# Chunked retention, a Strassen down product and 64-column matmul pairs in a fused retention + feed-forward kernel

## Chip, cores and metric

The kernel runs on one core of a Trainium2 chip. The metric is the device time in microseconds (us) of one execution. Only fast runs are compared (a run counts as slow when it is more than 1.5% above the fastest of the same kernel). Profiles show a span, from the first to the last instruction; where both are known for one execution, the timed value lies about 2 us above it.

Each result was timed against runs of the kernel before on the same chip, in the same rounds. A ratio is the mean time of one kernel's fast runs over the mean of the other's of the same rounds, so it is not quite the ratio of the medians that are quoted. Medians of different calls come from different chips; the kernel before had medians of 455.5, 454.2, 451.2 and 450.1 us in the four sets of rounds, so differences under about 1% between sets are not read.

## The reference

Eight batches, eight heads, 576 positions, head size 64; then a feed-forward block over 4,608 tokens of width 512 with 2,048 hidden units. All inputs and the output are float32. The product `g` is called the gate below.

```python
scores = scale * q @ k.T                       # per batch and head, 576 x 576
gamma  = 1 - 2.0 ** (-5 - arange(8))           # one per head
D      = where(i >= j, gamma ** (i - j), 0)    # causal decay
x      = ((scores * D) @ v)                    # to (4608, 512)
h      = x @ w_in                              # (4608, 2048)
g      = h * clip(h + 3, 0, 6) / 6
out    = g @ w_out                             # (4608, 512)
```

## The kernel before

Attention is quadratic. For each batch and pair of heads, q and k are loaded with a cast to fp16, transposed on TensorE (PE), and multiplied into a causal 576-wide triangle, which the Vector engine (DVE) multiplies by a precomputed decay mask. ACT is the Scalar engine, POOL the GpSimd engine, SP the engine whose queue issues stores and, in the changed kernel, most loads. In both kernels PE's outputs are tiles in the memory PSUM, and the other tiles lie in the memory SBUF. Feed-forward "units" are popped between the attention pieces to keep PE busy.

```python
# feed-forward, for a block of 512 tokens
for dmc in range(NCC):                                   # 4, up product (line 122)
    nc.tensor.matmul(ph, win16[:, dmc, P*fc:P*fc+P], xt16[:, dmc, tok0:tok0+512], ...)
nc.scalar.activation(u, ph, Relu, bias=0.5, scale=1/6)
nc.vector.scalar_tensor_tensor(out=gt16[:, fc, :], in0=u, scalar=1.0, in1=ph, op0=min, op1=mult)
...
for fc in range(NFC):                                    # 16, down product (line 136)
    nc.tensor.matmul(pout, gt16[:, fc, P*mc:P*mc+P], wout16[:, fc, :], ...)
nc.scalar.copy(osb, pout)
...
# attention, one pair of heads
nc.tensor.transpose(pst[...], nat[0:sj, j, :], ident16)  # q and k, 5 each (line 174)
nc.tensor.matmul(pms[h2][0:mt, ...], kt2[64*h2:64*h2+64, ...], qt2[64*h2:...])   # line 200
nc.vector.tensor_tensor(out=at16s[h2][...], in0=pms[h2][...], in1=dmask[...], op=mult)  # line 210
nc.tensor.matmul(pos[h2][64*h2:64*h2+64, ...], vn16[...], at16s[h2][...])        # line 230
```

The shape of the PE tile follows from the operands: lines 122, 136 and 174 use all 128 rows and 128 columns, line 200 uses 64 rows (two heads side by side), line 230 uses 64 columns.

## Time and profile before

| | kernel before |
|---|---|
| time | 455.52 us, median of 2 (454.57 to 456.48) |
| profiled span | 448.7 us |
| PE / DVE / ACT / POOL busy | 88% / 51% / 45% / 40% |
| feed-forward matmuls | 1,152 of 512 columns, one each 216 ns = 249 us |
| changes of PE tile shape | 381; at an estimated 96 ns each, 37 us |

These lines are from the page of the kernel before: the busy time of each engine, then PE's and the DMA engines' busy share in 40 slices (a digit is tenths), the DMA packets, the chain of work that ended last, and the largest group of matmuls (busy time, mean ns of one).

```profile
span 448.7 us, 6207 instructions
...
PE 394.0 (88%) x2368; PEld 181.7 (40%) x2368; DVE 230.5 (51%) x432; ACT 201.6 (45%) x349; POOL 177.6 (40%) x222
...
PE   0387999989998999899998999899989999899996
...
DMA packets 134700, 29.73 MB, mean 66 GB/s; under 512 B 126480, under 2 KB 130064, under 8 KB 134672
...
PE 69%; DVE 18%; ACT 9%; issue 2%; POOL 1%; DVEq 0%; POOLq 0%
...
L122 PE MATMUL ph<-xt_104,win_102 128*128 128x512 f16 x576 | 143.2, 383 | 5.7 <-DVE gt_1_955 L128 0.8
```

PE bounds the kernel, but 88% busy is not 88% useful. A matmul's 383 ns is a latency; what counts is the distance between starts, 216 ns for 512 columns. On the chain of work that ended last, DVE and ACT stand for a quarter of the span. The next lines, PE's timeline of the kernel before (start, duration, line, operation, count), show a loss that no share shows.

```profile
204.51 1.24 PE L122 MATMUL ph<-xt_104,win_102 128*128 128x512 f16 x5
205.68 0.31 PE L230 MATMUL po_2133<-at16a,vn_2048 128*64 128x288 f16 x1
205.69 0.31 PE L230 MATMUL po_2134<-at16b,vn_2048 128*64 128x288 f16 x1
```

The last of the five matmuls of line 122 starts at 205.37 (four times 216 ns after 204.51). The next start should be at 205.59 but is at 205.68: the tile shape changed from 128*128 to 128*64 and PE lost about 95 ns. The Trainium skill, "TensorEngine Tiling (Array Packing)", Key Properties, says that changing the tiling mode drains the engine; the trace agrees and gives the price. The second thing to see is that the two 64-column matmuls at 205.68 and 205.69 run at the same time, one in each half of the array's columns.

### The profile page before, as it was taken

The numbers are of one execution on the slowest core, as the hardware profiler recorded it, in microseconds if no ns is written. First come the engines' busy times: TensorE is split into PE (matmuls) and PEld (weight loads), VectorE is DVE, ScalarE is ACT, GpSimd is POOL, SyncE is SP. The second block draws the span as 40 slices with busy tenths as digits, with TensorE's granted clock in tenths as the row PEclk, the third lists the DMA queues.
The fourth block names the chain that finished last, engine by engine and source line by source line (L and its number), as shares of the span: only waits on it lengthen the run. The fifth ranks groups of instructions, "written<-read, shape, count | busy, mean of one in ns | idle before, by whom it ended". The sixth has DMA issues, their size and how long they took to land.

```text
span 448.7 us, 6207 instructions
## 1 busy us (share of the span) xinstructions
PE 394.0 (88%) x2368; PEld 181.7 (40%) x2368; DVE 230.5 (51%) x432; ACT 201.6 (45%) x349; POOL 177.6 (40%) x222
## 2 busy tenths in 40 slices
PE   0387999989998999899998999899989999899996
PEld 0133444434443444444443444344443444344442
DVE  0254675347716672467635771667245763480540
ACT  5623564156522663356415652266325641571641
POOL 9966799763534444155326353445200000000000
PEclk9999999999998999999999999999998999999999
DMA  5999999985777766487568568776210001001101
GB/s 36 123 189 192 120 96 96 154 75 37 46 92 88 46 45 61 86 55 50 37 101 74 39 44 93 87 50 42 39 70 1 0 1 70 26 0 48 47 23 70
DMA packets 134700, 29.73 MB, mean 66 GB/s; under 512 B 126480, under 2 KB 130064, under 8 KB 134672
## 3 DMA queue, kind: packets, MB, share of 16 engines
q0 software_dynamic: 129488, 19.91, 60.8%
q1 hardware_dynamic: 5184, 9.44, 5.7%
q8 instruction: 18, 0.29, 0.3%
q14 instruction: 10, 0.08, 0.1%
HBM read 39.80 MB, written 9.44 MB: 110 GB/s over the span
## 4 chain that ended last, share of the span: by engine, by line
PE 69%; DVE 18%; ACT 9%; issue 2%; POOL 1%; DVEq 0%; POOLq 0%
PE pout L136 28%; PE ph L122 22%; DVE at16a L210 8%; DVE at16b L210 6%; PE pst L174 5%; ACT dmask L80 3%; ACT xt_104 L236 2%; ACT u L126 2%; ACT sb L180 2%; DVE gt_6_3580 L128 1%; DVE gt_5_3055 L128 1%; DVE gt_0_430 L128 1%; DVE gt_4_2530 L128 1%; DVE gt_3_2005 L128 1%; DVE gt_2_1480 L128 1%
## 5 line engine op out<-in xcount | busy, mean ns | idle before, releaser
L122 PE MATMUL ph<-xt_104,win_102 128*128 128x512 f16 x576 | 143.2, 383 | 5.7 <-DVE gt_1_955 L128 0.8
L126 ACT ACTIVATE u<-ph,cb 128x512 f32<-128x512 f32 x144 | 97.2, 687 | 53.2 <-PE ph L122 51.0
L122 PEld LDWEIGHTS <-win_102 128*128 128x128 f16 x576 | 52.6, 97 | 71.0 <-issue 19.5
L140 ACT COPY osb<-pout 128x512 f32<-128x512 f32 x36 | 21.1, 585 | 111.5 <-PE pout L136 111.5
L178 DVE COPY sb<-pst 128x576 f16<-128x576 f16 x32 | 14.5, 455 | 43.3 <-PE pst L174 43.3
L200 PEld LDWEIGHTS <-sb 64*128 64x128 f16 (+1 forms) x384 | 14.9, 100 | 42.5 <-ACT sb L180 18.2
L180 ACT COPY sb<-pst 128x576 f16<-128x576 f16 x32 | 20.4, 637 | 3.6 <-PE pst L174 1.6
L128 DVE SCALAR_TENSOR_TENSOR gt_8_4320<-u,ph 128x512 f16<-128x512 f32 x16 | 11.0, 688 | 16.6 <-ACT u L126 16.6
L128 DVE SCALAR_TENSOR_TENSOR gt_6_3580<-u,ph 128x512 f16<-128x512 f32 x16 | 10.7, 681 | 9.0 <-ACT u L126 8.9
L128 DVE SCALAR_TENSOR_TENSOR gt_2_1480<-u,ph 128x512 f16<-128x512 f32 x16 | 10.5, 679 | 9.2 <-ACT u L126 9.2
L128 DVE SCALAR_TENSOR_TENSOR gt_5_3055<-u,ph 128x512 f16<-128x512 f32 x16 | 10.7, 681 | 8.0 <-ACT u L126 7.8
L128 DVE SCALAR_TENSOR_TENSOR gt_4_2530<-u,ph 128x512 f16<-128x512 f32 x16 | 10.7, 681 | 8.0 <-ACT u L126 7.8
L128 DVE SCALAR_TENSOR_TENSOR gt_0_430<-u,ph 128x512 f16<-128x512 f32 x16 | 10.5, 680 | 8.3 <-ACT u L126 8.3
L128 DVE SCALAR_TENSOR_TENSOR gt_1_955<-u,ph 128x512 f16<-128x512 f32 x16 | 10.5, 680 | 8.1 <-ACT u L126 8.1
L128 DVE SCALAR_TENSOR_TENSOR gt_3_2005<-u,ph 128x512 f16<-128x512 f32 x16 | 10.5, 680 | 8.1 <-ACT u L126 8.1
L136 PE MATMUL pout<-wout_103,gt_2_1480 128*128 128x512 f16 x64 | 14.3, 379 | 0.2 <-DVE at16a L210 0.2
L136 PE MATMUL pout<-wout_103,gt_4_2530 128*128 128x512 f16 x64 | 14.3, 379 | 0.2 <-DVE at16a L210 0.2
L136 PE MATMUL pout<-wout_103,gt_0_430 128*128 128x512 f16 x64 | 14.3, 379 | 0.2 <-DVE at16a L210 0.2
L136 PE MATMUL pout<-wout_103,gt_1_955 128*128 128x512 f16 x64 | 14.3, 379 | 0.2 <-DVE at16a L210 0.2
L136 PE MATMUL pout<-wout_103,gt_5_3055 128*128 128x512 f16 x64 | 14.3, 379 | 0.2 <-DVE at16a L210 0.2
L136 PE MATMUL pout<-wout_103,gt_6_3580 128*128 128x512 f16 x64 | 14.3, 379 | 0.2 <-DVE at16a L210 0.2
L136 PE MATMUL pout<-wout_103,gt_3_2005 128*128 128x512 f16 x64 | 14.3, 379 | 0.2 <-DVE at16a L210 0.2
(1059 smaller groups left out, 775.9 us busy)
## 6 DMA issues: line engine op xcount, KB each, us to landing
out_dram<-osb SPq DMA_DIRECT2D x36, 256.0 KB, 2.0
win_102<-in_moe_w_in_dram POOLq DMA_DIRECT2D x2, 640.0 KB, 8.8
wout_103<-in_moe_w_out_dram POOLq DMA_DIRECT2D x2, 640.0 KB, 10.0
win_102<-in_moe_w_in_dram POOLq DMA_DIRECT2D x1, 768.0 KB, 9.9
wout_103<-in_moe_w_out_dram POOLq DMA_DIRECT2D x1, 768.0 KB, 10.5
qn_108<-in_q_dram POOLq DMA_DIRECT2D x2, 80.0 KB, 3.0
kn_109<-in_k_dram POOLq DMA_DIRECT2D x2, 80.0 KB, 3.0
vn_110<-in_v_dram POOLq DMA_DIRECT2D x2, 80.0 KB, 3.1
```

What stands on the lines that cost most here:

```text
L80: nc.scalar.activation(dmask[:, h, :], rsel, ACTF.Exp, bias=cb[:, 1:2], scale=float(np.log(gamma[h])))
L122: nc.tensor.matmul(ph, win16[:, dmc, P * fc:P * fc + P], xt16[:, dmc, tok0:tok0 + MBLK], start=(dmc == 0), stop=(dmc == NCC - 1))
L126: nc.scalar.activation(u, ph, ACTF.Relu, bias=cb[:, 0:1], scale=1.0 / 6.0)
L128: nc.vector.scalar_tensor_tensor(out=gt16[:, fc, :], in0=u, scalar=1.0, in1=ph, op0=ALU.min, op1=ALU.mult)
L136: nc.tensor.matmul(pout, gt16[:, fc, P * mc:P * mc + P], wout16[:, fc, :], start=(fc == 0), stop=(fc == NFC - 1))
L140: nc.scalar.copy(osb, pout)
L174: nc.tensor.transpose(pst[:, P * j:P * j + sj], nat[0:sj, j, :], ident16[0:sj, 0:sj])
L178: nc.vector.tensor_copy(sb, pst)
L180: nc.scalar.copy(sb, pst)
L200: nc.tensor.matmul(pms[h2][0:mt, co:co + ns], kt2[base:base + D, P * tcix:P * tcix + mt], qt2[base:base + D, a:bb], start=True, stop=True)
L210: nc.vector.tensor_tensor(out=at16s[h2][0:mtg, alo:alo + wid], in0=pms[h2][0:mtg, 0:wid], in1=dmask[0:mtg, 2 * c + h2, alo:alo + wid], op= ...
L236: nc.scalar.copy(xt16[h2 * D:h2 * D + D, c, b * S + s0:b * S + s1], pos[h2][h2 * D:h2 * D + D, 0:s1 - s0])
```

## The change

Five things change at once:

1. **Attention by chunks.** 128 tokens of one batch are a unit, and consecutive units come from different batches. A unit multiplies only its own 128 x 128 scores; the past enters through a 64 x 64 state per head, updated once per unit. The decay becomes factors on q and v and a constant mask.
2. **Loads and transposes.** q, k, v come as fp32 by hardware-issued DMA in rows of 256 B and are cast on POOL (those of the first four units partly on DVE and ACT). From unit 8 on the transposes are DMA transposes.
3. **Strassen (Winograd's form) for the down product.** Seven half-size products per block (M1 to M7 in the code) instead of eight, with fp16 sums on DVE and evictions on ACT, DVE and POOL.
4. **Pairs.** Each 128-column matmul of the up and down products is issued as two matmuls of 64 columns, so nearly everything on PE has the tile shape 128*64.
5. **A fixed order** of events by steps. Each step holds one up group (128 hidden units of one block: four products of 512 columns), at most one half of a Strassen product, and on average a quarter of an attention unit.

The core of the diff, with cuts marked (`at_t(t, f)` puts the piece of work `f` at step `t`):

```diff
+    def mm2(o, l, r, start, stop):
+        for hf in (0, 64):
+            mm(o[hf:hf + 64], l[:, hf:hf + 64], r, start, stop)
...
-            nc.gpsimd.dma_start(dst[:, :, coloff:coloff + D], ap)          # cast to fp16
+                eng.dma_start(t[p0:p0 + nr], src[b, :, P * c:P * c + nr, :]
+                              .rearrange("h s d -> s h d"))                # fp32, on SP
...
+        nc.sync.dma_start_transpose(qT[u]..., qpad[u % NQ]...)
+        nc.sync.dma_start_transpose(kT[u], k16[u]...)
...
+    def pu(u):                                   # state update
+                mm(ps[64 * a:64 * a + 64, pr], k16[u][:, h], v16[u][:, h], pr == 0, True)
...
-                nc.tensor.matmul(pout, gt16[:, fc, P * mc:P * mc + P], wout16[:, fc, :], ...)
+    PROD = ["M1", "M2", "M4", "M6", "M5", "M7", "M3"]
+    def down(n, hp):                             # half hp % 2 of product hp // 2
+        tag = {"M1": "A", "M6": "A", "M7": "A", "M2": "B", "M4": "B", "M5": "D", "M3": "D"}[m]
+        new = m in ("M1", "M2", "M4", "M5")
+            acc[tag] = psum.tile([P, 2, 256], FP32, tag="acc" + tag, bufs=1, ...)
+        for j in range(8):
+            mm2(ps[:, mt], a[:, j, P * mt:P * mt + P], w[:, j, :], ...)
+        if m == "M2":
+            V(out=osb[n][0][:, :, 0:256], in0=ps, in1=snap["M1"], op=ALU.add)
...
+    DSTART = 24                                  # step of the first down product
+        if u >= 7:
+            at_t(tu - 9 - LEAD, lambda u=u: load(u))                       # LEAD = 10
```

## The prediction

> **What bounds the kernel now.** TensorE. The page's busy line gives PE 88% of a 448.7 us span; the chain of waits gives PE 69%, DVE 18%, ACT 9%. PE's busy share hides three things. (a) Successive matmul starts show the feed-forward part (1,152 matmuls of 512 columns) running at 216 ns each, 249 us: already full rate. (b) Whenever consecutive matmuls change the tile shape, the next start comes about 96 ns late (a 512-column matmul is followed after 312 ns instead of 216): 381 changes, about 37 us. This agrees with the Trainium skill, "TensorEngine Tiling (Array Packing)", Key Properties: changing the tiling mode drains the engine. (c) In each 48.4 us batch, PE waits for the retention chain (mask multiply of 0.68 us on DVE, copies on ACT): about 54 us over the run. The start is slow too: the first score matmul runs at 19 us.
>
> **What the change does to PE.**
> - Up product: 576 pairs of two 64-column tiles at 512 columns. Two column tiles already run concurrently in this trace (288-column pairs start 3 to 6 ns apart and follow after 122 to 126 ns), so 216 ns a pair: 124 us, unchanged.
> - Down product: Strassen, 7 products for 8: 9×14×8 = 1,008 pairs of 256 columns; estimate 256/2.4+3 = 109 ns: 110 us instead of 124.
> - Attention: chunk states replace the 576-wide triangle: per 128-token unit 8 score, 8 state and 16 output matmuls, about 1.1 us when paired, 40 us for 36 units; it was about 60 us plus drains. DMA transposes replace PE's from unit 8 on.
> - All work but the first 8 units' transposes has one tile shape, so nearly all drains go.
> PE sum: about 280 us.
>
> Doubling the weight loads should not bind: 64-column loads take 106 to 112 ns of latency against 97, but are prefetched; PE's sequencer already sustains load+matmul every 56 ns (transposes), 28 ns an instruction, and a down pair needs 4 per 109 ns. This is the tightest margin.
>
> **Other engines (estimates from the trace).** DVE: 144 gates × 0.68 = 98, 72 masks × 0.68 = 49, 72 Strassen sums of 1,024 fp16 elements, perhaps 0.6 each = 43, evictions and states 30, start 15: about 235 us, plus waits for the SBUF port that it shares with POOL (the skill's "SBUF — State Buffer", "SBUF: two separate sides"; not shown by this trace) of perhaps 25. ACT about 145. POOL about 190. So DVE runs some 80 to 90% busy in the steady part and will cause some PE stalls. DMA: 110,000 packets of 256 B; this trace sustains about 770 small packets/us: 145 us plus weights, outputs and transposes; not binding afterwards, but binding at the start: seven units and w_in share one queue, so up-projection should stall for late w_in parts and full pace comes only near 55 to 60 us.
>
> **Sum.** 58 (start, 16 up steps) + 128 steps × 1.9 us (240) + last 14 half products and store 17 = 315, plus 5% waits = 328 span; the timed value lies 7 us above the span before: **335 us, range 300 to 385**. Faster by over 2%: 0.95; within: 0.02; slower: 0.03.
>
> **Right or wrong would show as:** pair spacing of 216 (up) and 109 ns (down); 312 ns drain gaps gone; a thin PE row until about 55 us; PE over 85% busy thereafter, idle ended mostly by DVE; a final 14-us stretch without up work.
>
> **What would make it wrong:** pairs not concurrent at 256 columns, or PE bound by issuing four instructions a pair (down at 200 ns adds 90 us); DVE's fp16 sums at one element a cycle or blocked by POOL (adds 30 to 60); DMA transposes queued behind loads starving scores; single accumulators making PE wait for DVE in each block.

## The result, and the profile after

| | before | after |
|---|---|---|
| time, median of 2 | 455.52 us | 346.41 us (346.37 to 346.46) |
| ratio of fast runs, 95% interval | 1 | 0.764 (0.750 to 0.777) |
| span | 448.7 us | 344.8 us |
| PE / DVE / ACT / POOL busy, us | 394 / 231 / 202 / 178 | 297 / 239 / 150 / 162 |
| mean granted PE clock | 0.991 | 0.945 |
| DMA packets | 134,700 | 166,830 |

The page of the changed kernel, the lines that answer to those above, with the row of PE's granted clock and that of the DMA engines:

```profile
span 344.8 us, 10257 instructions
...
PE 297.1 (86%) x4352; PEld 235.8 (68%) x4352; DVE 238.6 (69%) x392; ACT 150.1 (44%) x235; POOL 162.4 (47%) x228
...
PE   3663929776999989999998999999999999999881
...
PEclk9965876989899999999999999999999999999997
DMA  9999999999998599899689979949999801100305
...
DMA packets 166830, 55.72 MB, mean 162 GB/s; under 512 B 158080, under 2 KB 160128, under 8 KB 166784
...
PE 65%; DVE 13%; DMA 9%; POOL 5%; issue 4%; ACT 2%; SPq 1%; DVEq 0%; POOLq 0%
...
L53 PE MATMUL up<-xt,win 128*64 128x512 f16 x1152 | 154.7, 390 | 2.3 <-DVE gt L283 2.3
```

PE's row shows three parts: ten uneven slices (86 us) in which the clock row dips and the DMA row stands at 9, then a full stretch, then a short end. The DMA row stays high after the start too (the share is 0.90 from step 24 to 122), so the row alone doesn't show that DMA bounds the start; runs 3 and 4 look into that. Measured in the steps of the schedule, by the first matmul of each up group in the trace:

| up step begins at, us | 0 | 16 | 24 | 122 | 143 | span ends |
|---|---|---|---|---|---|---|
| changed kernel | 33.4 | 66.7 | 83.2 | 284.2 | 321.2 | 344.8 |

The distances between single matmul starts are as forecast. The two halves of an up pair start 31 ns apart and the next pair follows 185 ns later, 216 in all; of a down pair 31 and 78, 109 in all.

So the total fits. Whether it fits for the forecast reasons is another matter. From step 24 to step 122 the trace lets one compare what PE had to stream with what it took: summing columns/2.4 ns over all matmuls (half for a 64-column one) gives 187.1 us of array time, in 201.0 us. (The 2.4 columns per ns is an estimate from the two spacings: 256 columns more take 216 - 109 = 107 ns more.) I call a start late when it comes over 15 ns after (columns/2.4 + 5) ns from the start before it, and sum the excess as "gaps": 8.7 us here, of which 6.7 lie in front of down products, and 4.95 in front of matmuls into the accumulator B alone. One of these gaps, in three timelines of the changed kernel (PE, DVE, POOL):

```profile
180.56 1.06 PE L53 MATMUL up<-xt,win 128*64 128x512 f16 x8
...
181.94 0.25 PE L53 MATMUL O<-qT,X 128*64 128x128 f16 x2
183.47 0.74 PE L53 MATMUL accB3M<-tw,gt 128*64 128x256 f16 x10 [1.28 <-DVE osb L350]
```

```profile
179.58 1.27 DVE L220 TENSOR_TENSOR at<-sc,maskc 128x512 f16<-128x512 f32 x2
180.78 1.45 DVE L295 TENSOR_TENSOR su<-gt 128x1024 f16<-128x1024 f16 x1
182.15 0.68 DVE L283 SCALAR_TENSOR_TENSOR gt<-u,up 128x512 f16<-128x512 f32 x1
182.74 0.68 DVE L350 TENSOR_TENSOR osb<-accB3M,snap3M 128x512 f32<-128x512 f32 x1
```

```profile
180.63 1.04 POOL L184 TENSOR_TENSOR v<-stgv,gv 128x512 f16<-128x512 f32 x1
```

M4 is the product that follows M2 and begins on the same single-buffered accumulator. It has to wait until DVE has read M2's result at line 350. DVE came late to that because its queue held two masks, an fp16 Strassen sum and a gate. And the sum took 1.45 us where such a sum takes 0.68: POOL was running, and the sum ended 0.55 us after POOL's record did. Of the 72 sums of this kind, 51 took 0.70 us or less and 21 took over 0.75, up to 1.53; all 21 began while a POOL operation ran, and they ended 0.55 us after it (the extra sums to 10.5 us). Of the other 51 only four began during a POOL operation, in its last 0.15 us. The Trainium skill, "SBUF — State Buffer", "SBUF: two separate sides", says that a DVE operation with two SBUF inputs and a POOL operation that reads SBUF exclude each other for a whole instruction; the trace agrees.

### The profile page after: what moved, and what is told of

It reads as the page before. It is cut to its first block, busy times and chain, and to the rows that moved or that the text cites. A ratio compares the mean times of both kernels' runs of the same rounds, so it can differ in the third digit from the quotient of the medians.

```text
span 344.8 us, 10257 instructions
## 1 busy us (share of the span) xinstructions
PE 297.1 (86%) x4352; PEld 235.8 (68%) x4352; DVE 238.6 (69%) x392; ACT 150.1 (44%) x235; POOL 162.4 (47%) x228
## 2 busy tenths in 40 slices
DMA packets 166830, 55.72 MB, mean 162 GB/s; under 512 B 158080, under 2 KB 160128, under 8 KB 166784
## 4 chain that ended last, share of the span: by engine, by line
PE 65%; DVE 13%; DMA 9%; POOL 5%; issue 4%; ACT 2%; SPq 1%; DVEq 0%; POOLq 0%
PE up L53 27%; DMA stgk<-in_k_dram 6%; PE sc L53 3%; DMA kT<-k 3%; PE O L53 3%; DVE su L295 2%; DVE at L220 2%; DVE gt L283 2%; PE tp L205 2%; POOL qpad L182 2%; PE accA8M L53 2%; PE accA6M L53 2%; PE accA2M L53 2%; PE accA7M L53 2%; PE accA4M L53 2%
## 5 line engine op out<-in xcount | busy, mean ns | idle before, releaser
L282 ACT ACTIVATE u<-up,cb 128x512 f32<-128x512 f32 x144 | 98.9, 687 | 136.8 <-PE up L53 129.4
L53 PE MATMUL up<-xt,win 128*64 128x512 f16 x1152 | 154.7, 390 | 2.3 <-DVE gt L283 2.3
L283 DVE SCALAR_TENSOR_TENSOR gt<-u,up 128x512 f16<-128x512 f32 x144 | 98.2, 683 | 64.6 <-ACT u L282 64.2
L53 PEld LDWEIGHTS <-win 128*64 128x64 f16 x1152 | 76.4, 113 | 31.7 <-issue 7.8
L53 PEld LDWEIGHTS <-su 128*64 128x64 f16 x1152 | 65.3, 110 | 9.5 <-issue 4.2
L53 PEld LDWEIGHTS <-gt 128*64 128x64 f16 x864 | 49.7, 111 | 11.7 <-issue 7.0
L220 DVE TENSOR_TENSOR at<-sc,maskc 128x512 f16<-128x512 f32 x64 | 41.0, 681 | 5.6 <-PE sc L53 5.6
L184 POOL TENSOR_TENSOR v<-stgv,gv 128x512 f16<-128x512 f32 x36 | 38.4, 1066 | 11.2 <-DMA stgv<-in_v_dram 11.1
L182 POOL TENSOR_TENSOR qpad<-stgq,gq 128x256 f16<-128x256 f32 x64 | 40.8, 658 | 0.0
L295 DVE TENSOR_TENSOR su<-gt 128x1024 f16<-128x1024 f16 x36 | 29.9, 831 | 0.0
L53 PE MATMUL O<-qT,X 128*64 128x128 f16 (+1 forms) x256 | 16.4, 213 | 0.0
```

Of the source, the lines that this page charges most:

```text
L53: nc.tensor.matmul(o, l, r, start=start, stop=stop, skip_group_check=True)
L182: eq.tensor_tensor(out=qp[:, :, a, 64 * a:64 * a + 64], in0=s[:, :, a, :], in1=bc(ga), op=ALU.mult)
L184: ev.tensor_tensor(out=v16[u], in0=stg["v", u], in1=bc(gv), op=ALU.mult)
L220: nc.vector.tensor_tensor(out=at[u][:, 2 * hf:2 * hf + 2].rearrange("p c a s -> p (c a) s"), in0=ps.rearrange("p c a s -> p (c a) s"), in1 ...
L282: nc.scalar.activation(ut, ph, ACTF.Relu, bias=cb[:, 0:1], scale=1.0 / 6.0)
L283: nc.vector.scalar_tensor_tensor(out=gt[n][:, fc, :], in0=ut, scalar=1.0, in1=ph, op0=ALU.min, op1=ALU.mult)
```

## Experiments

Two theories stood against each other.

- **A:** PE bounds the kernel from step 24 on, and DMA bounds it before. The chunked attention, without drains, is most of the gain; Strassen gives its 14 us of PE time; pairs give the drains.
- **B:** The saving of Strassen is lost to its own sums and accumulators; the start is bound by engines; the pairs cost as much as they save.

The answer is a mix of the two. In the tables "stretch" is up step 24 to 122, "array" and "gaps" as defined above. All three are worked out from the starts of single matmuls in the run's trace.

### 1. No pairs (e1_nopair)

```diff
-    PAIR = True
+    PAIR = False
```

> The changed kernel with each 128-column product of the up and down parts as one matmul again instead of two 64-column tiles (half the matmuls and weight loads there). Theory A, pairing pays only by avoiding drains: the attention matmuls stay 64 columns wide, so each of the 32 units from the fifth on brings 4 changes of tile shape, 128 in all at 96 ns (the figure of the kernel before): 12 us slower, about 358 us, ratio to the changed kernel 1.03 to 1.04; spacing of up and down matmuls unchanged at 216 and 109 ns. Rival B, the doubled loads (weight loads 68% busy) slow PE: same or faster, 335 to 346. Rival C, two tiles stream faster than one 128-column matmul: much slower, over 375.

Measured: 352.88 us (351.01 to 354.76), ratio to before 0.782 (0.776 to 0.788). Slower than the changed kernel by 6.5 us by the medians, by some 8 by the ratios (0.782 against 0.764): half to 70% of the 12 us that theory A expected. Spacing is unchanged at 216 and 109 ns, so neither rival holds: two tiles do not stream faster, and the doubled weight loads do not slow PE. PE's timeline of this run shows the drain that the pairs avoid:

```profile
148.00 1.03 PE L53 MATMUL up<-xt,win 128*128 128x512 f16 x4
148.96 0.63 PE L53 MATMUL sc<-qT,kT 128*64 128x256 f16 x8
149.52 1.05 PE L53 MATMUL accA2M<-wout,gt 128*128 128x256 f16 x8
```

The four up matmuls would let the score start at 148.86; it starts at 148.96, and 25 such starts come 309 ns after the last up matmul instead of 216. The stretch grows by 5.7 us at the same array time (187.1), not by the 9.4 us of 98 drains (24.5 units, four changes each). In front of accumulator B the gaps even fell (4.95 to 3.99): drains in front of down products fell partly where PE was waiting for DVE already.

### 2. Plain down product (e2_plain_down)

```diff
-            at_t(d + hp, lambda n=n, hp=hp: down(n, hp), 3)
-            ... ssum(...), wsum(...)                       # all fp16 sums
+            at_t(d + hp, lambda n=n, hp=hp: plain(n, hp), 3)
+    def plain(n, hp):
+        for x in range(64 * hp // 14, 64 * (hp + 1) // 14):
+            mt, fc = divmod(x, 16)
+            # one bank per 128 tokens, rotating over accA, accB, accD
+            mm2(acc["p"], gt[n][:, fc, P*mt:P*mt+P], wout16[:, fc, :], fc == 0, fc == 15)
+            if fc == 15: nc.scalar.copy(osb[n][mt // 2][:, mt % 2, :], acc["p"]); ...
```

The gate tile gets a third buffer, in the space of the sums, because a plain product keeps it longer.

> The changed kernel with the plain down product (64 pairs of 512 columns a block, spread over the same 14 slots, evicted by four copies on ACT, third gate buffer) in place of Strassen's; no fp16 sums. Theory A, PE bounds the steady part: 9 blocks times (64*216 - 112*109 ns = 1.6 us) = 14.6 us more PE work, so 8 to 15 us slower than the changed kernel, 354 to 361 us, with DVE busy falling by about 80 us. Rival B, Strassen's sums and evictions on DVE and its single accumulators cost as much as they save: within 1.5% of the changed kernel or faster. The final stretch without up work grows from about 16 to about 15+2 us.

Measured: 344.28 us (342.61 to 344.88), ratio 0.763 (0.758 to 0.768), against 0.764 for the changed kernel. Theory A fell: Strassen's seven products are no faster than eight plain ones. The two stretches side by side; each line gives the window, its length, then busy us and count for PE, weight loads, DVE, ACT and POOL, then PE clock, DMA share and GB/s. The first is of the changed kernel:

```profile
83.20:284.20 201.00, 195.44 (x3064) 162.32 (x3065) 159.01 (x249) 94.47 (x149) 111.37 (x140) 0.99 0.90 169
```

and this one of the plain form:

```profile
83.40:286.10 202.70, 201.92 (x2421) 120.42 (x2419) 104.87 (x171) 94.43 (x149) 92.01 (x134) 1.00 0.88 170
```

| | stretch | array | gaps |
|---|---|---|---|
| Strassen, as changed | 201.0 | 187.1 | 8.7 |
| plain | 202.7 | 198.4 | 1.0 |

The plain form streams 11.3 us more and takes 1.7 us more. DVE is busy 54 us less, and PE waits for almost nothing. The end is also longer with Strassen: the last up group is followed by 23.6 us, in the plain form by 19.6 (323.6 to 343.2). Whatever Strassen saves is given back in those two places. What remained open was whether it had to be.

### 3. Same bytes in larger packets (e3_big_packets)

```diff
-                eng.dma_start(t[p0:p0 + nr], src[b, :, P * c:P * c + nr, :]
-                              .rearrange("h s d -> s h d"))
+                eng.dma_start(t[p0:p0 + nr] as (p, 512),
+                              contiguous 2 KB per partition from the same batch)
```

The result is wrong (relative error 1.4): the bytes are the right ones in the wrong places.

> Wrong results on purpose: the q, k, v chunk loads read the same bytes as contiguous rows of 2 KB per partition instead of 8 rows of 256 B, so the same bytes come in an eighth of the packets. Theory A, the start is DMA-bound by packets (now one 1,024-packet load lands every 1.15 us and the first down matmul runs at 85.8 us): first down matmul at 60 to 70 us, total 322 to 332 us, steady spacing (29.4 us for 14 steps) unchanged. Rival B, the start is bound by engines (POOL casts, PE clock after idling): first down matmul still after 80 us, total above 340.

Measured: 335.33 us (334.77 to 336.18), ratio 0.744 (0.739 to 0.749). First the changed kernel's row of what its DMA engines moved, in 40 slices:

```profile
GB/s 173 229 300 256 225 247 222 205 208 167 198 152 126 131 217 191 198 202 179 102 213 189 197 197 204 180 104 194 151 169 233 124 2 63 63 2 3 124 3 122
```

and this run's, with its packets:

```profile
GB/s 244 393 386 344 279 247 174 188 177 108 143 120 127 250 209 128 237 187 122 131 278 202 116 239 224 70 185 167 164 171 223 64 2 67 63 2 16 114 2 127
DMA packets 70062, 55.72 MB, mean 167 GB/s; under 512 B 47488, under 2 KB 49536, under 8 KB 70016
```

In the first slices the same engines move up to 393 GB/s instead of 300, step 16 begins at 57.9 instead of 66.7 and step 24 at 71.9 instead of 83.2, and all of the 11 us stays in the total (the stretch is unchanged at 201.0). So DMA packets are a cost in the start, as theory A says, but a smaller one than it expected: the first down matmul runs at 74.4 us, not at 60 to 70, and the total is 3 us above its range. Step 0 begins at 33.1 us against 33.4, so none of the gain lies in the first 33 us; what bounds those this run does not show.

### 4. w_out loaded later (e4_wout_late)

```diff
-    for i in range(4): load_wout(i)                 # before step 0
+    for t, i in ((4, 0), (4, 2), (5, 1), (5, 3)):
+        at_t(t, lambda i=i: load_wout(i))
```

> The changed kernel with the four w_out loads issued from steps 4 and 5 on instead of before step 0, results correct. Theory A: in the changed kernel these loads hold up unit 5, unit 6 and the last w_in part between 27 and 48 us (PE idles 5.5 us before unit 6's transposes at 51 us); issued later they fill DMA time that nothing urgent needs: first down matmul 5 to 10 us earlier, total 336 to 342 us. Rival B: the start is bound by the sum of bytes to step 24 whatever the order: within 2 us of the changed kernel; or the sums of w_out now stall DVE and it is slower.

Measured: 347.40 us (346.46 to 348.14), ratio 0.770 (0.765 to 0.775): no gain, as rival B said (within 2 us). Step 16 came 10.7 us earlier (56.0 against 66.7), and step 20 at 76.0 against 76.1. So in the changed kernel the w_out loads do hold up the start: their packets run from 31.0 to 47.2 us, and in the ten us from 35 to 45 the queue of the other loads moves 1,290 packets, against 8,306 in this run; and step 0 begins at 33.4 us against 30.4 here. On the changed kernel's chain of work that ended last stand POOL's issuing of w_out and, after it, one load of a k chunk:

```profile
27.15 3.18 POOL wout L132 x4
34.21 15.62 DMA stgk<-in_k_dram
```

PE's longest wait between 54 and 84 us in this run:

```profile
PE sc L53 <- DMA kT<-k: 13.1, 1, 13.1
```

and the timeline of the SP queue, which issues both the loads and the transposes:

```profile
49.70 6.59 SPq L162 DMA_DIRECT2D stgv<-in_v_dram  x1
56.38 4.36 SPq L162 DMA_DIRECT2D stgq<-in_q_dram  x1
60.79 3.51 SPq L162 DMA_DIRECT2D stgk<-in_k_dram  x1
64.39 0.96 SPq L162 DMA_DIRECT2D stgv<-in_v_dram  x1
65.46 1.90 SPq L189 DMA_TRANSPOSE qT<-qpad  x1
```

The first transpose stands in one queue behind loads of units 10 and 11 that nobody needs yet, and these are held back by w_out (1,318 packets of that queue from 50 to 60 us, after 8,382 in the ten us before, while w_out's run from 49.4 to 63.7). It is issued at 65.5 us, in the changed kernel at 65.6: what stands ahead of it is the same in both. The gain turned into a new wait. It is the risk that the prediction named ("DMA transposes queued behind loads").

### 5 and 6. Another order of the seven products (e5_order), and its control (e6_start20)

```diff
-    PROD = ["M1", "M2", "M4", "M6", "M5", "M7", "M3"]
+    PROD = ["M1", "M2", "M6", "M5", "M7", "M4", "M3"]     # e5 only
-        if m == "M7": ... nc.gpsimd.tensor_tensor(... snap["M7"], snap["M4"], subtract); store(n, 1)
+        if m == "M4": nc.gpsimd.tensor_tensor(... snap["M7"], snap["M4"], subtract); store(n, 1)
-    DSTART = 24
+    DSTART = 20                                           # e5 and e6
```

In the old order M4 follows M2 on accumulator B, and M3 is separated from M5 on accumulator D only by M7, whose end is what the read of D waits for. In the new order each accumulator rests for one whole product.

> The changed kernel with the seven Strassen products in the order M1 M2 M6 M5 M7 M4 M3, so that a product never starts on the accumulator that the product just before it filled; the pool subtraction for the fourth quarter follows M4; the down part starts at step 20 instead of 24 so that gate tiles are released in time. Theory A, Strassen's PE saving is lost to waits on single accumulators (in the changed kernel 8.7 us of excess gaps before accumulator and score matmuls between up steps 24 and 122, and both kinds of down product take 201 to 203 us there): those gaps fall under 3 us, the stretch from up step 24 to 122 falls from 201 to 192 to 195 us, total 334 to 340 us. Rival B, the fp16 sums keep DVE late whatever the order: gaps move to other matmuls, stretch above 199 us, total within 2 us of the next run.

> Control for the run before: the changed kernel with its own product order, only the down part starting at step 20 instead of 24. Theory A: the four half products that now run in the DMA-bound start give at most 4*0.87 = 3.5 us, total 342 to 346 us; the gaps before accumulator matmuls stay at 8 to 10 us. Rival B (the start step explains what the reordered kernel gains): total 334 to 340 us.

Measured, on the same chip: the new order 336.53 us (336.36 to 336.95), the control 343.96 us (342.70 to 344.95). Below are PE's waits from 86 us on in the changed kernel (engine, waiter, what it waited for: us in total, times, longest):

```profile
PE accB8M L53 <- DVE osb L350: 1.4, 1, 1.4
PE accD8M L53 <- DVE osb L352: 1.4, 1, 1.4
PE accB3M L53 <- DVE osb L350: 1.3, 1, 1.3
PE accB1M L53 <- DVE osb L350: 1.3, 1, 1.3
PE accB0M L53 <- DVE osb L350: 0.8, 1, 0.8
...
PE sc L53 <- DMA kT<-k: 0.3, 1, 0.3
```

and from 80 us on with the new order:

```profile
PE sc L53 <- DMA kT<-k: 1.0, 2, 0.7
PE sc L53 <- ACT u L282: 0.7, 1, 0.7
```

| | stretch | array | gaps | of these before accumulators |
|---|---|---|---|---|
| control (start at step 20) | 195.7 | 183.7 | 7.6 | 6.5 |
| new order | 191.0 | 183.7 | 3.1 | 0 |

The waits for accumulators are gone and the kernel is 7.4 us faster, though 17 of the 72 sums still ran into POOL. Both totals of theory A hold, and rival B of each falls; of the finer figures, the gaps came to 3.1 us where under 3 were expected, the stretch to 191.0 where 192 to 195 were, and the control's gaps before accumulators to 6.5 where 8 to 10 were. DVE has the same 392 operations in both runs (234.6 and 236.7 us busy). So about half of Strassen's gain, 7.4 of an estimated 14 us of PE time, had been lost to the order in which its products reuse three accumulators, and not to the mere amount of DVE work. Where the other half goes these two runs don't show; run 8 shows a part of it.

### 7 and 8. A lighter start, with the plain product (e7_plain_start) and with the reordered one (e8_order_start)

```diff
+    for i in range(4): at_t(0, lambda i=i: load_wout(i))   # instead of before step 0
-    LEAD = 10
+    LEAD = 4                                                # loads 13 steps ahead, not 19
-    DSTART = 24
+    DSTART = 16
+    ... at_t(DSTART + (0, 1, 3, 5)[i], wsum(i, ...))        # e8 only
```

> Plain down product as in the second run of the first call, and a lighter start: w_out loads issued at step 0, chunks of q, k, v prefetched 13 steps ahead instead of 19 (LEAD 4), down part from step 16. Theory A, DMA limits the start, and loads queued ahead of need delay what is needed: up step 24 at 70 to 76 us although 8 half products are done by then (83 us with none in the plain run), total 324 to 332 us. Rival B, the start is bound by the sum of bytes or by POOL: up step 24 at 83 us or later, and the total gains only the 8 half products, 336 to 344 us.

> Strassen in the reordered form and the same lighter start (w_out loads at step 0, LEAD 4, down part from step 16, sums of w_out from step 16 on). Theory A (accumulator waits and DMA order are separate losses that add): 318 to 328 us, below the plain form of the run before by 3 to 10 us. Rival B, Strassen never pays on this chip because DVE carries its sums: equal to or slower than the plain form.

Measured: plain 335.83 us (333.81 to 338.21), reordered Strassen 329.64 us (328.05 to 330.86), on the chip of runs 5 and 6.

The plain form fell between the two ranges, at the edge of rival B's 336 to 344. Up step 24 began at 81.1 us, against 83.4 in run 2, with eight half products already done (an estimated 0.99 us each, 64/14 pairs of 216 ns, 7.9 in all). If the half products cost nothing in the slow start, they are most of the gain of 8.5 us, and the new loads earned about 2. That split is argued: the loads and the earlier down part changed together, and no run parts them. What the loads alone reach is step 16, before which no down product runs: 61.4 us against 67.2 in run 2, and in the Strassen form 61.7 against 67.5 in run 5.

For Strassen, step 24 began at 85.4 us with eight half products done, in run 5 at 86.3 with four, so of the 5.8 us gained at step 16 one is left: from there to step 24 run 8 takes 4.8 us more than run 5, 3.4 of them array time of the four more half products. Runs 7 and 8 have the same loads and show what holds Strassen up there: from step 16 to 24 the plain form takes 19.7 us and Strassen 23.7, though it has less array time there (15.6 against 16.4). The window from 60 to 80 us in run 7, then in run 8 (DVE is the third busy time):

```profile
60.00:80.00 20.00, 16.94 (x208) 9.92 (x209) 10.41 (x18) 8.50 (x14) 11.36 (x17) 1.00 1.16 196
```

```profile
60.00:80.00 20.00, 14.72 (x216) 10.65 (x216) 19.59 (x30) 8.43 (x13) 14.31 (x17) 1.00 1.10 184
```

DVE, which has the sums of w_out and of the gates here, is busy all the time with Strassen and half of it in the plain form, at a similar DMA share. Strassen in the new order is now 6.2 us below the plain form, as theory A said (its total is 1.6 us above the range of 318 to 328); its stretch has 180.3 us of array time, 186.8 long, with gaps of 2.3.

### 9. All transposes on PE (e9_pe_transposes)

```diff
-        at_t(tu - 6 if u >= 8 else tu - 1, lambda u=u: (tr if u >= 8 else trpe)(u))
+        at_t(tu - 1, lambda u=u: trpe(u))
```

> The changed kernel with PE transposes for all 36 units (12 transposes, one DVE and one ACT copy a unit) in place of DMA transposes from unit 8 on. Theory A, PE bounds the steady part: 28 units times (12*56 + 2 changes of tile shape*96 = 0.86 us) = 24 us more PE work, total 366 to 374 us. Rival B: DVE, ACT and PE have room, and the 43,000 packets less on the DMA engines shorten the start: below 356 us.

Measured: 365.07 us (364.77 to 365.80), ratio 0.812 (0.810 to 0.813): 18.7 us slower than the changed kernel by the medians (some 22 by the ratios), near theory A's range and far from rival B's. The stretch has 15.4 us more array time and is 18.1 us longer. Up step 24 began at 84.0 us, so the packets saved did not help the start; only four units' transposes are issued before step 24 in the changed kernel, the first at 65.6 us.

### 10. Only the attention (e10_attention_only)

This is run 2 with `PAIR = False`: plain down product, 128-column matmuls, everything else as changed.

> The changed kernel with plain down product and without pairs: of the change only the chunked attention, its loads, DMA transposes and schedule remain. Theory A: these carry nearly all of the gain, and pairs are worth the 5 to 9 us of saved drains: 349 to 354 us. Rival B: pairs and Strassen together carry a good part: over 365 us.

Measured: 355.18 us (354.19 to 356.93), ratio 0.790 (0.787 to 0.793). The chunked attention with its loads and schedule takes the kernel from 450.1 to 355.2 us; pairs then take it to 344.3 (ratio 0.763), and Strassen as written adds nothing. The time is 1.2 us above theory A's range, far below rival B's. What the first 95 us consist of, only run 9 looks into (the transposes). An estimate from the traces: array time falls from 302.1 to 283.3 us (matmuls of 64 rows counted half too), 18.8 us, and there are 136 changes of tile shape instead of 381, at 96 ns another 23.5 us. The rest, some 52 us, is other waiting of PE, and no run parts chunks from schedule there. Here pairs are worth some 11 us, more than in run 1: the stretch is 212.8 against 202.7 us at the same 198.4 us of array time. With the plain product the profile shows no wait of PE for another engine after 86 us, in this run or in run 2, so every drain counts; with Strassen as written some drains hide in waits.

### 11. A shorter end (e11_tail)

```diff
+                eng = nc.scalar if n == NB - 1 and p0 else nc.sync     # last block's stores
+            e = nc.vector if n == NB - 1 else nc.gpsimd                # last subtraction
```

> The reordered Strassen kernel with the lighter start (329.6 us), and in the last block the stores of the lower 64 rows issued from ACT's queue instead of all eight from SP's (which takes 5 us), and the last subtraction on DVE instead of POOL (1.27 us). Expected 325.5 to 328.5 us; if the end is bound by the transfers and not by issuing, no change (329 to 331).

The SP queue at the end of run 8, then of this one:

```profile
321.18 5.04 SPq L322 DMA_DIRECT2D out_dram<-osb  x8
```

```profile
319.06 2.48 SPq L323 DMA_DIRECT2D out_dram<-osb  x4
```

Measured: 325.50 us (325.06 to 327.45), ratio 0.724 (0.722 to 0.727), at the edge of the expected range. But run 8 is of another set: by the ratios (0.724 against 0.728) the gain is 0.5%, less than is read between sets. What the traces show is the end: the last up group is followed by 19.7 us instead of 21.7. Which of the two edits earned that, no run parts. This version has the lowest median, and its result is correct.

### 12. Keeping PE's clock up (e12_warm)

```diff
+    def warm(n):
+        ps = psum.tile([P, P], FP32, tag="accA", bufs=1, name=f"warm{n}")
+        for _ in range(n): mm2(ps, ident, ident, True, True)
+    at_t(-2, lambda: warm(50)); at_t(9, lambda: warm(60), 3); at_t(15, lambda: warm(35), 3)
```

> The run before plus 145 pairs of dummy matmuls of 128 columns at three places of the start where PE waited 2.5 to 4.2 us for loads (granted clock there 0.74 to 0.83), results correct. Theory A, the low clock is a consequence: loads pace the start, so the total stays within 2 us of the run before although the granted clock rises. Rival B, the low clock costs: 4 to 7 us faster.

The window from 20 to 60 us in run 11 (the clock is the third figure from the end):

```profile
20.00:60.00 40.00, 30.13 (x308) 18.98 (x309) 26.49 (x39) 19.19 (x29) 24.17 (x34) 0.91 1.12 232
```

and in this run:

```profile
20.00:60.00 40.00, 35.53 (x622) 25.76 (x622) 27.24 (x46) 20.86 (x32) 24.15 (x34) 1.00 1.10 229
```

Measured: 326.98 us (324.96 to 329.13): no gain. Step 16 came at 58.9 instead of 61.7 us, and step 24 at 85.5 in both. The low clock in the start follows from the waiting (it rises from 0.91 to 1.00 when dummy work fills the waits) and costs nothing that the total shows. Run 11's own profile happened to have a clock of 0.91 where run 8's had 0.79, and their step 24 differed by 0.1 us too, which says the same.

## Why the prediction was right, and where not

The time (335 forecast, 346.4 measured) lies in the range and the direction was right. That alone says little: every run, from 325 to 365 us, lies in the range of 300 to 385, and the plain product gives the same time, so that the total fits is in part luck. Point by point:

- **PE bounds it, drains go, pairs stream at 216 and 109 ns:** right, read from the starts (15 changes of tile shape are left, all in the start). Issuing four instructions in 109 ns was no limit.
- **Attention:** about 40 us was forecast for 36 units; the array time is 32.4 us for all, 23.3 in the stretch. Right in kind, a little generous.
- **"Down product: Strassen ... 110 us instead of 124":** true of the array, and worth nothing in the time of this kernel. This is the step that failed as an argument: in the sum it hid behind the other estimates. Run 2 shows that the plain form is as fast, and runs 5 and 6 that the cause of about half of the loss is the risk listed last, "single accumulators making PE wait for DVE in each block".
- **DVE:** 235 us forecast, 238.6 measured; a sum of 1,024 fp16 elements takes 0.68 us instead of 0.6, and the shared port added 10.5 us where 25 were allowed. The Trainium skill, "VectorE: DVE Perf Modes", Mode 2×_1P, says that two packed 16-bit values are handled at a time; the trace agrees: 0.68 us is also what 512 fp32 elements from PSUM took. ACT 145 against 150. POOL 190 against 162.
- **The sum's three terms.** Up step 16 was to begin at 58 us and began at 66.7: this is the largest mis-sized term. The prediction named seven units and w_in as the start's loads and left out w_out: with w_out later, step 16 begins at 56.0 (run 4), with larger packets for q, k and v at 57.9 (run 3). The count of 110,000 small packets also left out 43,000 that the DMA transposes add (153,600 packets of 256 B in the trace), but the first of these is issued at 65.6 us, so they did not delay step 16. The 128 steps were to take 240 us plus 13 of waits and took 255.4 (to 322.1): right, but with less attention work and more waiting than thought. The end was to take 17 us and took 22.7: the last block's two accumulator waits of 1.4 us and SP issuing eight stores for 5 us. The misses are 8.7, 2.4 and 5.7 us, and make up the 16.8 between the forecast span of 328 and the measured 344.8. The 7 us added for the timed value were too many: it lies 1.7 us above the span.
- **"PE idle ended mostly by DVE" after the start:** right.

What stays open: after the lighter start, step 24 still begins at 85 us in runs 8, 11 and 12. Run 7 beside run 8 puts some 4 us of that down to Strassen's sums on DVE. The plain form's 81.1 us, and the first 30 to 34 us before step 0 in all runs, no run explains: DMA's share is as high there as where PE runs full (1.16 from 60 to 80 us in run 7, and 1.16 from 80 to 100 too).

## What to carry to other kernels

A saving in the work of the bounding engine counts only as far as the engine doesn't have to wait for the helpers that the saving needs: compare its streaming time with the elapsed time of a stretch before and after, and undo the saving once on its own. When products share few accumulators, order them so that no product starts on one that the product just before it filled. Mixed tile shapes on PE cost some 96 ns at a change here, and splitting full-width matmuls into pairs of half-width ones removed the changes at no cost in streaming (216 and 109 ns with and without). Before a count of packets is blamed for a late step, look when those packets run.

## What the Trainium skill lacked or had wrong

- "TensorEngine Tiling (Array Packing)", Key Properties, names the drain on a change of mode but gives no price: here about 96 ns each (a 512-column matmul followed after 309 to 320 ns instead of 216), at 381 changes in the kernel before.
- The same page, Performance Considerations, advises column tiling for products of at most 64 columns. Here full 128-column products gained from it too, with unchanged spacing (216 and 109 ns), because the shape then stays the same: 6 to 8 us with Strassen, some 11 without. Its Restrictions say that column tiling turns Fast Weight Load off; the 64-column loads do take 110 to 113 ns against 97 for full ones, and it cost nothing here.
- "SBUF — State Buffer", "SBUF: two separate sides": the exclusive port is as stated. What it lacks is a size in a real kernel: sums of 0.68 us stretched to as much as 1.53, 21 of 72, 10.5 us of DVE time.
- "DMA: Bandwidth & Descriptors", "DMA Transpose (X-bar)": the section does not say what transposes inside SBUF cost in packets. Here one unit (128 x 1,536 fp16 elements) took 1,536 packets of 256 B, half of what the unit's loads took (3,072), and they queue with them.
